# Fast matrix products in the second half of a feed-forward, and a leaner convolution transform beside them

## The chip, the cores and the metric

The kernel runs on one core of one Trainium2 chip. The metric is the device time of one execution in microseconds (us). The kernel before takes 1298.86 us, the median of three runs (1296.42 to 1302.47).

Five engines work side by side, each through its own queue in order: TensorE (PE in the profile) multiplies matrices, VectorE (DVE) and ScalarE (ACT) do elementwise work, GpSimd (POOL) issues DMAs that add to memory, SyncE (SP) issues plain DMAs. The order of each queue is fixed when the kernel is built.

## The reference

`x` is 2048 rows by 1024 columns, `F` is 3584. Two branches are summed onto `x`:

```python
xn = _layernorm(x)
# branch A, per channel, along the 2048 rows
kv  = short_causal_conv(k, shift_k, 4 taps) * v
y   = irfft(rfft(kv, 4096) * rfft(ssm_k, 4096))[:2048] + kv * ssm_D
A   = xn * y
# branch B
B   = silu(xn @ w1) @ w2        # 1024 -> 3584 -> 1024
out = x + A + B
```

All of it is float32 to the outside. The kernel multiplies matrices in float16 parts: each operand is split into a high and a low half, and a product takes three matrix multiplications (high by high, high by low, low by high).

## The kernel before, in words

**The feed-forward** has two halves. The first (`xn @ w1`, then silu) works on pairs `i` of 128-column tiles of `F` (14 pairs) and on four blocks `b` of 512 rows. Pairs 0 and 1 are partly done plainly (`plain_unit`). The rest go through `units` (line 795): two row blocks by two column tiles by two halves of the depth are a 2 by 2 block product, done with seven products in place of eight (Winograd's form; `PRODUCTS` names the seven left and right factors). The factors of `xn` and `w1` are sums formed beforehand. A unit is seven runs of 12 matmuls (P1, P7, P6, P2, P5, P3, P4), in three banks of PSUM; `evacuate` (line 722) copies parts between them with ScalarE and adds two with VectorE, and `block` (line 704) applies silu, splits the result into float16 halves (`split`, line 276: one ScalarE and one VectorE instruction) and stores it in DRAM (`hs`).

The second half (`h @ w2`) is plain in the kernel before (lines 841 to 879): for two halves `h` of 512 output columns and sixteen row tiles `t`, 28 tiles of `F` by three matmuls of 512 columns (lines 868 to 870) build one bank. `load_h` (line 903) brings `hs` back into the ring `wo`, and `norms_w2`/`load_w2` (lines 938 and 971) bring `w2`, split it with the factor `tau` and put it into the eight large `places`, which the first half has used before. `result` (line 895) copies a finished bank out with ScalarE and adds it to `out` with an accumulating DMA of GpSimd (`G`, line 250).

**The convolution** (`convolution`, line 989) runs over eight groups `g` of 128 channels beside the feed-forward. `gate` forms `kv` on VectorE. `signal_parts` transposes and splits it. `stage1` (line 1105) multiplies by the transform's constants `cfw`: for each of four `t` and two `c`, two products `p0`, `p1` of three matmuls go into two PSUM tiles, and `to_spec` (line 1137) makes their sum and difference, with one ScalarE copy and two VectorE operations. `forward`, `product` (line 1186) and `inverse` are VectorE work on the tile `spec`: butterflies, the complex product with the filter's transform, butterflies back. `energy` sums the squares for a scale. `result_parts` splits into `zh`, `zl`, `stage1_inv` (line 1317) multiplies by `civ` into the PSUM tile `py`, and `gated` (line 1338) multiplies by the normalised rows on VectorE into one of two buffers `yt`, which two accumulating DMAs of 128 KB each add to `out`. `spec` and `tmp` are single tiles, so a group's transform cannot start before the group ahead has given them up.

**The order of the work.** The class `Order` is a planner that runs at build time. Every piece is a generator that yields operations; each has an engine, a cost, a latency, a margin `m` that is kept between the end of what it reads and its own start, and a bias of its stream. The planner takes the operation that can start first, less its bias, and appends it to its engine's queue. `Ring` hands out buffers when the planner's clock frees them. A plain or accumulating DMA is priced with a fixed latency and a common pipe; an accumulating one (`G`) holds GpSimd for 1.1 us in the plan. On the chip the queues run in that order, whatever the real durations are. `places` are the eight large tiles that hold the factors of `xn`, then `w2`; the last result of the kernel waits for the convolution's results in the plan and leaves by a plain DMA (`last_result`, line 882).

Of the kernel before, what the change touches and what calls it, by code (L numbers as in the profile page):

```python
# [11 lines left out]
F32 = mybir.dt.float32  # L12
# [30 lines left out]
W2PLACE = [(5, 4, 2, 7, 6, 3, 0), (1, 5, 4, 2, 7, 6, 3)]  # L43
# [142 lines left out]

class Ring:
# [25 lines left out]
def h3_ffn_kernel(ctx, tc, x, kp, vs, fs, shift, dskip, w1, w2, cfwd, cinv, out):  # L213
# [70 lines left out]
    dram = ctx.enter_context(tc.tile_pool(name="dram", bufs=1, space=bass.MemoryType.DRAM))  # L284
    hs = [dram.tile([4, P, NF, 2, P], F16, name=f"hs{b}") for b in range(4)]
# [10 lines left out]
    wsc = cst.tile([P, NP, 4], F32, name="wsc")  # L296
    e1s = wsc[:, :, 3]
    powers = cst.tile([P, 4], F32, name="powers")
    for n, e in enumerate((14 - 64, 10 - 64, 64 - 23, 64)):
        nc.vector.memset(powers[:, n:n + 1], 2.0 ** e)  # L300
# [310 lines left out]
    def scales_w1():  # L611
        for n, (_, i) in enumerate(pairs):
# [14 lines left out]
            def then(e, i=i):  # L627
                sc = wsc[:, i]
                nc.vector.tensor_scalar(sc[:, 2:4], powers[:, 2:4], e, None, op0=MUL)
                nc.vector.reciprocal(e, e)  # L630
                nc.vector.tensor_scalar(sc[:, 0:2], powers[:, 0:2], e, None, op0=MUL)
# [71 lines left out]

    def block(i, b, j, src, tok):

        if src.space == bass.MemoryType.PSUM:
            yield hfs.ready
            hf, htok = hfs.tile([P, 4, P])
            yield a_act(hf, src, AF.Silu, wsc[:, i, 2:3])
            tok.set()  # L710
        else:
            hf, htok = src, tok
            yield a_act(hf, src, AF.Silu, wsc[:, i, 2:3])
# [81 lines left out]
    def units():  # L795
# [5 lines left out]
        for n, (i, sp) in enumerate(todo):  # L801
            if sp == 1:
                flag["unit", i].set()
            made, seen = defaultdict(Token), defaultdict(Token)
# [36 lines left out]
    def feed_forward():  # L841
# [9 lines left out]
        second["tok"].set()  # L851
        yield from units()
        flag["gemm1"].set()
        for h in range(2):
            for t in range(NT):
                yield ff.ready
                po, tok = ff.tile([P, W])
                final = (h, t) == (1, NT - 1)
                if final:
                    add(last_result(h, t, po, tok), EB)  # L860
                for c in range(NF // 4):
                    yield flag["h", h, t, c]
                    hx, htok = flag["h", h, t, c].what
                    yield flag["w2", h, c]
                    wc, wtok = w2c[h, c]
                    for jj in range(4):
                        def mm(jj=jj, j=4 * c + jj):
                            nc.tensor.matmul(po, hx[:, jj, 0, :], wc[:, jj, 0, :], start=(j == 0), stop=False)  # L868
                            nc.tensor.matmul(po, hx[:, jj, 0, :], wc[:, jj, 1, :], start=False, stop=False)  # L869
                            nc.tensor.matmul(po, hx[:, jj, 1, :], wc[:, jj, 0, :], start=False, stop=(j == NF - 1))  # L870
                        yield T(mm, po, [hx[:, jj], wc[:, jj]], 3 * 0.2185)
                    htok.set()
                    if t == NT - 1:
                        wtok.set()
                if final:
                    flag["last"].set()
                else:
                    add(result(h, t, po, tok), EB)

    flag["conv out"] = Token(NG * 4 * 2)  # L880

    def last_result(h, t, po, tok):

        yield flag["conv out"]
        yield hfs.ready
        o, otok = hfs.tile([P, W])
        to = orr[t // T2, t % T2, :, h * W:(h + 1) * W]
        yield L(o, to)
        yield flag["last"]
        yield v_stt(o, po, invc[:, 0:1], o, MUL, ADD)  # L890
        tok.set()
        yield L(to, o)
        otok.set()
# [9 lines left out]
    def load_h():  # L903
        yield flag["factors"]
        for h in range(2):
            for t in range(NT):
                for c in range(NF // 4):
                    yield wo.ready
                    flag["h", h, t, c].what = o, _ = wo.tile([P, 4, 2, P], F16)
                    yield L(o, hs[t // 4][t % 4][:, 4 * c:4 * c + 4])  # L910
                    flag["h", h, t, c].set()
# [26 lines left out]
    def norms_w2():  # L938
# [10 lines left out]
        def then(e):  # L949
            nc.vector.tensor_scalar(invc, e, 2.0 ** (64 - 25), None, op0=MUL)  # L950
            nc.vector.reciprocal(cc, e)
            nc.vector.tensor_scalar(tau, e1s, 2.0 ** (15 - 64), cc, op0=MUL, op1=MUL)
        yield from norm(ctxs["nm"], qs, (1,), then, ([invc, tau, cc], [flag["tau"]]))
        add(load_w2(), 0.05)
        for h in range(2):
            for c in range(NF // 4):
# [6 lines left out]
                for a in range(4):  # L963
                    j = 4 * c + a
                    yield lambda: bool(w2raw)
                    raw, tok = w2raw.pop(0)
                    add(split(wc[:, a, 0, :], wc[:, a, 1, :], raw, tau[:, j // 2:j // 2 + 1], (tok, flag["w2", h, c])), 0.05)

    w2raw = []

    def load_w2():
        for h in range(2):
            for j in range(NF):
                r = (ctxs["wraw"], ctxs["w2n"], hfs)[j % 3 if h == 1 and j > 3 else j % 2]
                yield r.ready
                raw, tok = r.tile([P, W])
                yield L(raw, w2r[:, j, h * W:(h + 1) * W])
# [484 lines left out]
```

## Time and profile before

| | before |
|---|---|
| median of three runs, us | 1298.86 |
| the profiled execution, us | 1299.35 |
| span of the profile, us | 1297.6 |
| mean granted TensorE clock | 0.993 |
| PE busy, share of the span | 98% |
| DVE busy | 1145.9 us, 88% |
| ACT busy | 691.9 us, 53% |
| POOL busy | 98.4 us, 8% |
| first half's last matmul starts | 607.8 us |
| second half's first matmul starts | 608.1 us |

The profile is one execution on the chip. A group of instructions is given by source line, engine, operation, the tiles it writes and reads, its shape, its count, its summed time, the mean of one in nanoseconds, and the idle time of the engine ahead of it with what ended it. Matmuls are pipelined, so the 380 ns of one matmul is its latency, and the distance from start to start is shorter. VectorE's instructions overlap a little as well.

### The profile page before, as it was taken

To read this page: it belongs to the slowest core of one execution; us is meant where nothing else is said; L and a number is where in the kernel's file an instruction comes from. 1 tells how busy PE (TensorE), PEld (TensorE's weight loads), DVE (VectorE), ACT (ScalarE), POOL (GpSimd) and SP (SyncE) were. 2 spreads that over 40 slices of the span, in tenths; PEclk is the share of its full clock that TensorE was granted. 3 is DMA by queue.
4 is the path that set the end of the run, shared out by engine and by line. 5 is a ranking of instruction groups with operands and counts; after the bars stand their busy time and mean duration, and the time that the engine had idled before them with its cause. 6 is when DMAs were issued, how large, how long until landed. Compare 5 with 4: busy or idle time off the path is not lost.

```text
span 1297.6 us, 17976 instructions
## 1 busy us (share of the span) xinstructions
PE 1268.9 (98%) x6242; PEld 618.4 (48%) x6242; DVE 1145.9 (88%) x1758; ACT 691.9 (53%) x1238; POOL 98.4 (8%) x101
## 2 busy tenths in 40 slices
PE   7899999999999998999999999999999999999998
PEld 6444544444444543445444544544544454454453
DVE  8999997889999759999899899899899989989920
ACT  6867987887766856768523412512562252241120
POOL 0000000000000011001100200210110021011021
PEclk8999999999999998999999999999999999999999
DMA  9456899789998879869954664674596367456462
GB/s 324 163 163 211 291 318 311 255 263 348 323 324 284 273 214 285 262 207 296 294 168 100 148 186 136 151 191 129 137 290 190 97 156 190 111 112 133 114 138 33
DMA packets 207003, 269.93 MB, mean 208 GB/s; under 512 B 15416, under 2 KB 121920, under 8 KB 204480
## 3 DMA queue, kind: packets, MB, share of 16 engines
q1 hardware_dynamic: 185040, 252.26, 60.7%
q0 software_dynamic: 21872, 16.52, 10.3%
q8 instruction: 49, 0.80, 0.2%
q14 instruction: 42, 0.34, 0.1%
HBM read 193.22 MB, written 83.89 MB: 214 GB/s over the span
## 4 chain that ended last, share of the span: by engine, by line
PE 71%; DVE 17%; DMA 6%; issue 4%; ACT 2%; POOL 0%; SPq 0%; DVEq 0%; ACTq 0%; POOLq 0%
PE ff L763 12%; PE ff L761 12%; PE ff L762 12%; PE ff L869 9%; PE ff L870 9%; PE ff L868 9%; DVE spec L255 5%; DVE tmp L255 3%; DVE acc L258 2%; DMA out<-yt 2%; DMA kin<-in_kp 1%; DVE x L258 1%; PE ps L1127 1%; PE ps L1129 1%; PE ps L1128 1%
## 5 line engine op out<-in xcount | busy, mean ns | idle before, releaser
L869 PE MATMUL ff<-x,wo 128*128 128x512 f16 x896 | 340.7, 380 | 1.3 <-DVE x L258 1.3
L868 PE MATMUL ff<-x,wo 128*128 128x512 f16 x896 | 340.5, 380 | 0.8 <-ACT x L266 0.8
L870 PE MATMUL ff<-x,wo 128*128 128x512 f16 x896 | 340.5, 380 | 0.0
L761 PE MATMUL ff<-x,wo 128*128 128x512 f16 (+1 forms) x808 | 305.1, 378 | 5.7 <-ACT v L266 4.2
L762 PE MATMUL ff<-x,wo 128*128 128x512 f16 (+1 forms) x808 | 305.0, 377 | 2.1 <-DVE x L258 2.1
L763 PE MATMUL ff<-x,wo 128*128 128x512 f16 (+1 forms) x808 | 304.8, 377 | 2.1 <-DVE wo L258 2.1
L255 DVE TENSOR_TENSOR spec<-spec 128x512 f32<-128x512 f32 (+2 forms) x192 | 219.4, 1175 | 1.3
L870 PEld LDWEIGHTS <-wo 128*128 128x128 f16 x896 | 87.7, 98 | 107.7 <-issue 2.4
L868 PEld LDWEIGHTS <-wo 128*128 128x128 f16 x896 | 88.6, 99 | 101.1 <-issue 0.8
L869 PEld LDWEIGHTS <-wo 128*128 128x128 f16 x896 | 87.7, 98 | 102.2 <-issue 1.7
L252 POOL DMA_DIRECT2D out<-yt x64 | 70.5, 1102 | 810.2 <-DMA w2n<-in_w 430.9
L763 PEld LDWEIGHTS <-wo 128*128 128x128 f16 x808 | 79.4, 98 | 99.5 <-DVE wo L258 4.7
L762 PEld LDWEIGHTS <-wo 128*128 128x128 f16 x808 | 79.4, 98 | 92.4 <-issue 6.4
L761 PEld LDWEIGHTS <-wo 128*128 128x128 f16 x808 | 80.6, 100 | 88.5 <-ACT wo L266 2.1
L255 DVE TENSOR_TENSOR tmp<-spec 128x512 f32<-128x512 f32 (+1 forms) x112 | 100.3, 915 | 0.2
L258 DVE SCALAR_TENSOR_TENSOR ht<-hf,wsc,ht 128x512 f16<-128x512 f32 x112 | 83.4, 746 | 17.9 <-ACT ht L266 17.6
L266 ACT ACTIVATE ht<-hf,wsc 128x512 f16<-128x512 f32 x112 | 80.9, 722 | 3.6
L258 DVE SCALAR_TENSOR_TENSOR acc<-kin,taps,acc 128x512 f32<-128x512 f32 x96 | 71.7, 747 | 2.1 <-ACT acc L266 1.9
L266 ACT ACTIVATE xg<-xg,nmr,rstd 128x128 f32<-128x128 f32 x128 | 54.8, 482 | 34.9 <-DMA xg<-in_x 33.5
L266 ACT ACTIVATE zh<-spec,csc 128x1024 f16<-128x1024 f32 x32 | 36.1, 1142 | 66.4 <-DVE spec L258 49.1
L266 ACT ACTIVATE yt<-spec 128x1024 bf16<-128x1024 f32 x32 | 33.7, 1053 | 67.6 <-DVE spec L255 67.4
L266 ACT ACTIVATE v<-ff,invc 128x512 f32<-128x512 f32 x31 | 21.2, 683 | 89.5 <-PE ff L870 89.5
(151 smaller groups left out, 1756.2 us busy)
## 6 DMA issues: line engine op xcount, KB each, us to landing
wo<-hs SPq DMA_DIRECT2D x224, 256.0 KB, 3.0
hs<-ht SPq DMA_DIRECT2D x112, 256.0 KB, 4.6
ws<-wo SPq DMA_DIRECT2D x84, 256.0 KB, 3.6
wo<-ws SPq DMA_DIRECT2D x84, 256.0 KB, 3.7
w2n<-in_w SPq DMA_DIRECT2D x80, 256.0 KB, 4.7
raw<-in_w SPq DMA_DIRECT2D x28, 512.0 KB, 5.5
kin<-in_kp SPq DMA_DIRECT2D x32, 448.0 KB, 3.7
xt<-in_x SPq DMA_DIRECT2D x16, 512.0 KB, 7.2
```

Source lines behind the costliest of these rows:

```text
L252: return Op("POOL", 1.1, 4.0, lambda: nc.gpsimd.dma_start(o, i, accum_op=ADD), [i], [o], m, n)
L255: return V(lambda: nc.vector.tensor_tensor(o, a, b, op=op), o, [a, b], **k)
L258: return V(lambda: nc.vector.scalar_tensor_tensor(o, a, s, b, op0=op0, op1=op1), o, [a, b] + ([] if isinstance(s, float) else [s]), **k)
L266: nc.scalar.activation(o, i, func, scale=scale, **kw)
L761: nc.tensor.matmul(o, w[:, 0, k], xf[:, :, k, 0], start=first and k == 0, stop=False, **kw)
L762: nc.tensor.matmul(o, w[:, 0, k], xf[:, :, k, 1], start=False, stop=False, **kw)
L763: nc.tensor.matmul(o, w[:, 1, k], xf[:, :, k, 0], start=False, stop=last and k == KH - 1, **kw)
L868: nc.tensor.matmul(po, hx[:, jj, 0, :], wc[:, jj, 0, :], start=(j == 0), stop=False)
L869: nc.tensor.matmul(po, hx[:, jj, 0, :], wc[:, jj, 1, :], start=False, stop=False)
L870: nc.tensor.matmul(po, hx[:, jj, 1, :], wc[:, jj, 0, :], start=False, stop=(j == NF - 1))
L1127: nc.tensor.matmul(ps, cf[:, 0, cs], hi[:, i], start=True, stop=False)
L1128: nc.tensor.matmul(ps, cf[:, 0, cs], lo[:, i], start=False, stop=False)
```

## The change

It has three parts.

**Fast products in the second half.** The pairs 6, 7, 8 and 9 of the 14 (eight of the 28 tiles of `F`) are taken out of the plain sum. For them the 2 by 2 blocks are two row blocks, the two tiles of a pair, and the two halves of the output columns; each of eight tiles `u` of 128 rows by two takes seven runs of 12 matmuls (`units2`). The left factors are sums of silu's results: `quad` forms them with four VectorE additions and seven splits per pair and row half, in place of four splits, and stores them in `hsf`. Silu's results wait in a tile taken from place 4 (first row half) and place 5 (second). The right factors are sums of `w2` blocks, formed in `norms_w2` after the plain part's `w2`, from raw blocks loaded again where they are needed twice. `evacuate2` empties the banks: four results per `u` go to `out` by accumulating DMAs, beside one for each of the 32 plain tiles, now of 20 tiles of `F`. The plain tiles `t` 0 and 1 of the first column half, and 14 and 15 of the second, are computed together.

**Convolution.** In stage 1 both products of a pair go into one PSUM tile, the second on top of the first; ScalarE copies twice the first before, and their sum after, and VectorE makes the difference: two ScalarE copies and one VectorE operation in place of one and two. `product` does its multiplications in four instructions of 2048, 512, 512 and 1024 elements in place of seven (one of 1024, six of 512), and `energy` writes its unused squares into `spec`, no longer into a `yt` buffer.

**Hops.** The margin of the stage 1 matmuls, forward and inverse, is 1.0 in place of 2.0; `py` may take a spare feed-forward bank, the split parts may take an `ht` buffer once the first half is over, and spare banks end with the plain part (`last part`).

In core, cut at "...":

```diff
+PAIRS = (6, 7, 8, 9)
+PLAIN = [j for j in range(NF) if j // 2 not in PAIRS]
+NC = len(PLAIN) // 4
+W2PLACE = [(5, 4, 2, 7, 6), (3, 0, 1, 5, 4)]
+FPLACE = (2, 7, 6, 3, 0, 1, 5, 4)
...
+    def quad(i, sp):
+        def factor(name, hf, tok=None):
+            yield hts.ready
+            ht, ttok = hts.tile([P, 4, 2, P], F16)
+            yield from split(ht[:, :, 0, :], ht[:, :, 1, :], hf, wsc[:, i, 2:3], () if tok is None else (tok,))
+            yield L(hsf[sp][name][:, :, PAIRS.index(i)].rearrange("q p h s -> p q (h s)"), ht.rearrange("p q h s -> p q (h s)"))
...
+        yield v_tt(v, z, v, ADD)
+        add(factor("S1", v, vt), 0.03)
+        yield v_tt(z, x, z, SUB)
+        add(factor("S3", z, zt), 0.03)
+        yield v_tt(x, v, x, SUB)
+        add(factor("S2", x, xt), 0.03)
+        yield v_tt(y, y, x, SUB)
+        add(factor("S4", y, yt), 0.03)
...
+    def units2():
+        def product2(n, u, o, first=False):
+            yield flag["h2", u, n]
+            hx, htok = flag["h2", u, n].what
+            yield flag["w2f", n]
+            wc, wtok = w2f[n]
+            yield from steps2(o, hx, wc, first, True, not first)
...
+    def evacuate2(u, one, c, made, seen):
+        def copied(src, tok, to):
+            yield hfs.ready
+            o, otok = hfs.tile([P, W])
+            yield a_act(o, src, AF.Copy, invc2[:, 0:1])
+            tok.set()
+            yield G(to, o)
+            otok.set()
...
+        yield a_act(d, two, AF.Copy, invc2[:, 0:1])
+        seen["P5"].set()
+        yield v_stt(d, c[0], invc2[:, 0:1], d, MUL, ADD)
+        seen["P7"].set()
+        yield G(at(u, 1, 1), d)
...
+        yield v_stt(a, c[0], invc2[:, 0:1], a, MUL, ADD)
+        c[1].set()
+        yield L(at(u, 1, 0), a) if last else G(at(u, 1, 0), a)
...
+        for k, (name, (_, of)) in enumerate(PRODUCTS.items()):
+            r = places[FPLACE[k + 1]]
+            yield r.ready
+            wc, wtok = w2f[name] = r.tile([P, NQ, 2, W], F16)
...
+                if of == "T3":
+                    b12, t12 = yield from next_w2()
+                    yield v_tt(src, raw, b12, SUB)
...
+                elif of == "T4":
+                    yield v_tt(src, raw, src, SUB)
...
+                elif of == "T1":
+                    b11, t11 = yield from next_w2()
+                    yield v_tt(raw, raw, b11, SUB)
...
-            yield a_act(total, p0, AF.Copy)
-            tok0.set()
-            yield v_tt(diff, total, p1, SUB)
-            yield v_tt(total, total, p1, ADD)
-            tok1.set()
+            yield a_act(diff, ps, AF.Copy, 2.0)
+            seen.set()
+            yield made
+            yield a_act(total, ps, AF.Copy)
+            yield v_tt(diff, diff, ps, SUB)
+            tok.set()
...
+                yield v_tt(run(tmp, 0, 16), steps_of(xx, 0, (2 * P, 4), (0, 4)), run(k, 0, 4, (4 * P, 2), (0, 2)), MUL)
+                for s in range(2):
+                    yield v_tt(steps_of(k, (4 * s + 3) * P, (-P, 2), (-2 * P, 2)),
+                               steps_of(xx, (4 * s + 3) * P, (0, 2), (-2 * P, 2)),
+                               steps_of(k, (4 * s + 2) * P, (-2 * P, 2), (0, 2)), MUL)
+                o = steps_of(tmp, P, (2 * P, 8))
+                yield v_tt(o, o, run(k, 0, 8), ADD)
...
-                    yield py_r.ready
-                    py, tok = py_r.tile([P, 2, 2, P])
+                    yield lambda: py_r.ready() or spare()
+                    py, tok = (py_r if py_r.ready() else ff).tile([P, 2, 2, P])
...
-                        yield T(mm, py[:, :, i, :], [hi[:, i], lo[:, i]], 0.66, m=2.0)
+                        yield T(mm, py[:, :, i, :], [hi[:, i], lo[:, i]], 0.66, m=1.0)
```

How the queues change, counted in the order of the two kernels: TensorE has 96 matmuls of 512 columns fewer. VectorE has, of 512 elements, 64 additions fewer in stage 1 and 128 multiplications or additions fewer in `product` (which has 32 more of 2048 instead), and 16 more additions on `w2` and 32 in `quad`; 24 more splits in `quad`, 12 more on `w2`, and 16 in `evacuate2`. GpSimd has 63 accumulating DMAs of 256 KB in place of 31, beside the same 64 of 128 KB.

More of the change, by code (lines that the diff above doesn't have):

```diff
@@ L854, in feed_forward @@
         for h in range(2):
-            for t in range(NT):
-                yield ff.ready
[L857 to L878, printed above, removed]
```

349 lines of the change are left out of this document (260 added, 89 removed).

## The prediction, made before the changed kernel was run

> **What bounds the kernel now.** I read first the page's line of busy times, then the stretches of the span, to see which engine has room in which stage.
>
> ```profile
> PE 1268.9 (98%) x6242; PEld 618.4 (48%) x6242; DVE 1145.9 (88%) x1758; ACT 691.9 (53%) x1238; POOL 98.4 (8%) x101
> ```
>
> ```profile
> 0.00:150.00 150.00, 135.07 (x719) 74.58 (x720) 141.33 (x317) 116.44 (x201) 0.69 (x6) 0.98 0.67 224
> 150.00:608.00 458.00, 452.65 (x2185) 215.62 (x2184) 411.02 (x643) 348.17 (x635) 13.36 (x12) 0.99 0.89 283
> 608.00:1237.00 629.00, 624.54 (x3056) 300.45 (x3054) 587.22 (x793) 220.40 (x392) 73.81 (x73) 1.00 0.62 162
> 1262.00:1290.00 28.00, 28.00 (x131) 12.63 (x130) 0.00 (x0) 0.69 (x1) 3.98 (x4) 1.00 0.30 44
> ```
>
> Behind the stretch's length stand the busy times of PE, weight loads, DVE, ACT and POOL with counts, then the granted clock, the DMA share and GB/s. PE has work throughout. In the last row 131 matmuls of 512 columns, alone, take 28.0 us, so one costs 0.2155 us (28 by 130 distances), although its own latency is 0.38. DVE idles 9, 47 and 42 us in the first three stretches, and has nothing to do after 1258. So PE sets the time now, with DVE close behind. Second I read the waits and the places where PE lost time.
>
> ```profile
> PE ff L761 <- ACT v L266: 4.2, 1, 4.2
> DVE yt L258 <- DMA out<-yt: 22.0, 5, 6.9
> ```
>
> ```profile
> 488.00:500.00 12.00, 7.80 (x24) 2.80 (x22) 11.97 (x15) 8.87 (x20) 2.87 (x3) 0.72 1.05 278
> 960.00:985.00 25.00, 22.88 (x99) 9.80 (x98) 24.88 (x31) 12.79 (x23) 1.75 (x2) 0.93 0.86 284
> ```
>
> One wait of 4.2 us at 489 drops the clock to 0.72 over 12 us: it costs 4.2 plus half of some 6 us, 7 in all. At 960 to 985, the turn between the two column halves, PE loses 2.1 us and 0.07 of 25 us more: 4. Third I read the end.
>
> ```profile
> 1239.75 1.11 POOL L252 DMA_DIRECT2D out<-yt  x1 [3.77 <-DVE yt L258]
> 1244.08 1.09 POOL L252 DMA_DIRECT2D out<-yt  x1 [3.22 <-issue]
> ...
> 1268.24 1.09 POOL L252 DMA_DIRECT2D out<-yt  x1 [2.50 <-issue]
> 1268.83 1.42 POOL L252 DMA_DIRECT2D out<-v  x1
> ```
>
> ```profile
> 1147.94 0.75 DVE L258 SCALAR_TENSOR_TENSOR yt<-py,csc,xg 128x512 f32<-128x512 f32 x1 [0.42 <-PE py L1333]
> ...
> 1166.02 0.75 DVE L258 SCALAR_TENSOR_TENSOR yt<-py,csc,xg 128x512 f32<-128x512 f32 x1 [2.53 <-PE ff L870]
> ```
>
> ```profile
> 1238.58 0.75 DVE L258 SCALAR_TENSOR_TENSOR yt<-py,csc,xg 128x512 f32<-128x512 f32 x1 [2.98 <-PE py L1333]
> ...
> 1256.03 0.75 DVE L258 SCALAR_TENSOR_TENSOR yt<-py,csc,xg 128x512 f32<-128x512 f32 x1 [6.90 <-DMA out<-yt]
> 1293.66 0.75 DVE L258 SCALAR_TENSOR_TENSOR hf<-ff,invc,hf 128x512 f32<-128x512 f32 x1 [36.88 <-PE ff L870]
> ```
>
> A group's eight accumulating DMAs go one by one, 4.07 us apart (28.5 by 7), though the instruction holds POOL for 1.1. With two buffers, a group's fourth gate (`yt`) follows the first by 17 to 18 us. At the kernel's end this is hidden now: the last group's eight are issued by 1268, PE ends at 1293.6, and 4.0 us for one addition and one plain DMA make the span.
>
> **The change, part by part.**
>
> *TensorE.* 96 matmuls less at 0.2155: **-20.7 us**. Stage 1 and the inverse keep their matmuls.
>
> *The turn at 960.* Of five pieces of the second `w2` half only two, not six, wait for places that the first half still holds. I take **-4**, bounds -4 and 0.
>
> *VectorE, in total.*
>
> ```profile
> L255 DVE TENSOR_TENSOR spec<-spec,ps 128x512 f32<-128x512 f32 x73 | 49.9, 684 | 9.1 <-PE ps L1129 7.1 <-ACT spec L266 1.1
> L258 DVE SCALAR_TENSOR_TENSOR ht<-hf,wsc,ht 128x512 f16<-128x512 f32 x112 | 83.4, 746 | 17.9 <-ACT ht L266 17.6
> L255 DVE TENSOR_TENSOR spec<-spec 128x2048 f32<-128x2048 f32 x24 | 54.9, 2287 | 0.4
> L255 DVE TENSOR_TENSOR tmp<-spec 128x1024 f32<-128x1024 f32 x48 | 58.3, 1221 | 0.2
> ```
>
> ```profile
> 1196.81 1.29 DVE L255 TENSOR_TENSOR spec<-tmp 128x512 f32<-128x512 f32 x2
> ```
>
> Two additions of 512 take 1.29 us together, one 0.69, so behind another one costs 0.60; by the same overlap a split's half costs 0.66, an operation of 1024 1.14, of 2048 2.2. Stage 1: 64 by 0.60, -38.4. `product`: 7 operations (1.14 + 6 by 0.60 = 4.74) become 2.2 + 1.2 + 1.14 = 4.54, 32 times: -6.4. Added: 48 additions, 28.8; 36 splits, 23.8; 16 results, 10.6. **Net +18 us of VectorE**, in a span that is to be 21 shorter; bounds +12 (if the strided forms overlap more) and +25. By place: in the order of the queues, VectorE's work ahead of the last addition of the first half sums to 575 us (before 553, beside 552 busy by 608 in the rows), against a TensorE queue of 580 (before 575). VectorE's idle time up to there, 56 us before, must shrink to 38 or PE waits. Part of the 56 is waits that quads can fill (the 17.6 above is a wait for ScalarE), part is gates waiting for the DMAs. I take **+5**, bounds 0 and 17.
>
> *ScalarE* gets some 80 us more; in the row of 608 to 1237 it is idle for 409 us, and in the first half, 348 of 458, the cover is thinner. I cost it at nothing; if it is late, its price falls under the +5, since the same queues meet there.
>
> *The first fast tile.* The seven right factors are split last, while stage 1 of group 7 and the product of group 6 go on. In VectorE's new queue, between the scale reduction of group 7's input (which waits for a small matmul) and the last split of T4 stand 13 operations of 512, two of 1024, one of 2048, 17 split halves or the like and seven small ones at 0.16: 7.8 + 2.3 + 2.2 + 11.3 + 1.1 = 24.7 us. TensorE's queue between that small matmul and the use of T4 (P4 of the first `u`) holds 84 matmuls and 12 transposes: 18.1 + 1.3 = 19.4. So PE waits 5 us there at least, if VectorE is on time at the start. It will not be: group 5's four gates stand ahead, with only 7 us of VectorE work among them in the new queue, and the rows above give them 17 to 18. The raw blocks, 36 where the plain form loads 16, come through four buffers. A wait of this length also costs clock, as at 489. I take **+10**, bounds 5 and 20.
>
> The Trainium skill, in "TensorE: Matmul & The Clock Gate", section "The HAM clock gate", says that an idle window of some 3.4 us sends the clock to half. The trace agrees: the 4.2 us wait above is followed by a clock of 0.72. By that rule two waits of 3 us here would cost 6 and not 10.
>
> *The end.* In the new TensorE queue the last group's first inverse block begins 22 us ahead of the queue's end (56 before), and its last block is followed by 42 matmuls, 9 us (192 before, 41). So the first accumulating DMA starts 22 less 1.3 (the block), 0.3, 0.75 (the gate) and 0.4 ahead of PE's end E: E - 19. Eight of them take 28.5 to the last issue. Behind them in the new queue stand three of 256 KB from the last `u`.
>
> ```profile
> out<-yt POOLq DMA_DIRECT2D x64, 128.0 KB, 4.1
> out<-v POOLq DMA_DIRECT2D x31, 256.0 KB, 4.4
> ```
>
> The first follows the last `yt` at once, as at 1268.83; whether two more fit is not shown. If they do: 0.6 + 0.9 + 0.9 + 4.4 = 6.8 to the last landing; if they wait for a landing, 9.5. I take 8. The end is E - 19 + 28.5 + 8 = E + 17 against E + 4 now: **+13**, bounds +5 (the inverse placed as now, only the three behind) and +17.
>
> The Trainium skill, in "DMA: Bandwidth & Descriptors", section "Anatomy of one DMA — SWDGE (gpsimd) path", fits 2.0 us plus the bytes by 436 GB/s to one DMA from GpSimd: 2.3 us for 128 KB. By that estimate the eight would end some 12 us sooner and the time be near 1291. The rows differ: 4.07.
>
> *ScalarE's wider share of stage 1, the hops at 1.0.* A shorter margin can only bring a matmul closer to what it waits for. The stage 1 matmuls wait for nothing in the rows of before; I cost the margin at nothing, bounds -2 and +6, the latter one wait of about 1 us per group.
>
> **Sum:** -20.7 - 4 + 5 + 10 + 13 = +3.3 us. The profiled execution took 1299.35 (its span 1297.6 and 1.75 around it), 0.5 above the median of 1298.86. So I forecast **1303 us**: nothing gained, the saving given back at the first fast tile and by GpSimd's queue at the end.
>
> **The rivals.**
>
> *The saving comes through in part.* VectorE keeps up (its 42 us of idle time in the long stretch absorb the waits), and the first fast tile costs at most a few us. Then the first two gifts stay and only the end gives back: 1299.35 - 20.7 - 4 + 13 = **1288**. For it speaks that PE waited hardly at all in 600 us of such order before; against it that the 24.7 and 19.4 above are counts.
>
> *VectorE becomes the bound.* The gates decide it. With 7 us of work between the first and the fourth gate where they take 17 to 18, VectorE stands 10 to 11 us per group; before, the 18.1 us from first to fourth gate held some 13 of work by the order, so 5. For groups 2 to 6 that is 5 by 6 = 30 us more standing, on top of the 18 of work. PE is spared as long as VectorE's lead covers it; the lead fell by 17 at the end of the first half, so it decides from there on. If half of the 30 reaches PE: 1303 + 15 = **1318**. For it speaks the 6.90 in the last gate's row, and the 4.2 at 489, which came by way of such a gate; against it, that most of TensorE's queue behind the gates is feed-forward that needs nothing of VectorE.
>
> *The accumulating DMAs overlap.* POOL holds each for 1.1 us, so at the least eight would start within 9 us in place of 28.5, and the end would be E + 4 again: 1303 - 13 = 1290. The rows of 4.07 speak against it; I give it 0.05, counted with the saving in part.
>
> *The change doesn't do what it says.* It does: the counts of the matmuls, stage 1 additions and product operations stand in the queues. What it can fail to do is make the hops shorter, since the margin sits in the plan and the gates in GpSimd's DMAs; then the group time stays at some 100 us and the sum above is unchanged.
>
> **How the numbers follow.** The forecast's own range, 1296 to 1311, has half of the chance; the saving in part (1278 to 1296) 0.25; VectorE as the bound (1311 to 1330) 0.25. 0.5% is 6.5 us, about what a measurement of this kernel can tell from no change: 1292.4 to 1305.4 counts as the same. Below it lie four fifths of the second case, 0.20; above it the third case and two fifths of the first, 0.45; between them 0.35. The range that leaves out a tenth on each side goes from 1286 (the second case, with the bound of 5 us at the end taken half) to 1320 (the third, a little above its price).
>
> **What would show it.** In the profile of the changed kernel: 6146 matmul records or so and VectorE busy for 1158 to 1171 us; PE waiting for VectorE on an `x` tile (the factors of `w2`) or on the last group's transposes for 5 us or more, at the first fast tile, with the clock below 1 behind it; the eight `out<-yt` of the last group some 4 us apart, the first about 19 us ahead of PE's last matmul; the last event of the span an `out<-hf` DMA of GpSimd, 12 us or more after PE's last matmul. It would be wrong if the last event were again the plain DMA 4 us after PE; if PE had no wait over 3 us in the second half; or if the accumulating DMAs came closer than 3 us.

## The result, and the profile after

The changed kernel takes **1316.51 us** (median of four runs, 1314.44 to 1317.76) against 1299.55 us (four runs, 1296.42 to 1302.47): ratio 1.0127, 95% interval 1.011 to 1.0144. It is 17 us slower. The forecast was 1303, its range 1286 to 1320.

The page's line of busy times of the kernel after:

```profile
PE 1255.1 (96%) x6146; PEld 610.2 (46%) x6146; DVE 1166.1 (89%) x1701; ACT 769.4 (59%) x1379; POOL 126.3 (10%) x133
```

The 96 matmuls are gone and VectorE has 20 us more work, yet the span grew by 15.0, from 1297.6 to 1312.6. The stretches of the kernel after (columns as in the prediction):

```profile
150.00:613.00 463.00, 452.72 (x2174) 215.42 (x2173) 424.61 (x645) 360.50 (x666) 13.35 (x12) 0.99 0.89 286
613.00:1237.00 624.00, 611.45 (x2976) 292.52 (x2975) 558.41 (x689) 272.28 (x482) 92.95 (x95) 0.99 0.71 183
1128.00:1142.00 14.00, 7.86 (x36) 3.42 (x35) 14.00 (x19) 9.01 (x15) 1.74 (x2) 0.95 0.82 222
960.00:985.00 25.00, 25.00 (x118) 11.33 (x116) 22.65 (x23) 7.14 (x16) 6.17 (x6) 1.00 0.80 174
1237.00:1313.00 76.00, 55.78 (x283) 27.44 (x280) 41.87 (x52) 20.25 (x32) 19.29 (x20) 0.90 0.58 98
```

The turn at 960 to 985 now has PE busy for all of its 25 us: that stall is gone. At the first fast tile (1128 to 1142) PE works 7.86 of 14 us while VectorE works all 14. In the last 76 us PE is busy for 55.78. The waits of the kernel after (engine, line, who ended the wait; us in total, times, longest):

```profile
PE py L1581 <- DVE yt L285: 5.7, 2, 3.6
...
PE ff L976 <- DVE x L285: 3.3, 5, 1.1
PE px L1355 <- DVE ht L285: 3.2, 1, 3.2
...
DVE yt L285 <- DMA out<-yt: 30.4, 6, 7.0
```

VectorE stands 30.4 us (22.0 before) at gates whose buffer an accumulating DMA still holds. The timeline of the kernel after at its end, first VectorE's last gates, then GpSimd's queue:

```profile
1271.73 0.75 DVE L285 SCALAR_TENSOR_TENSOR yt<-py,csc,xg 128x512 f32<-128x512 f32 x1 [0.43 <-PE py L1583]
...
1275.63 0.75 DVE L285 SCALAR_TENSOR_TENSOR yt<-py,csc,xg 128x512 f32<-128x512 f32 x1
1283.40 0.75 DVE L285 SCALAR_TENSOR_TENSOR yt<-py,csc,xg 128x512 f32<-128x512 f32 x1 [7.01 <-DMA out<-yt]
1290.78 0.75 DVE L285 SCALAR_TENSOR_TENSOR yt<-py,csc,xg 128x512 f32<-128x512 f32 x1 [6.63 <-DMA out<-yt]
```

```profile
1272.93 1.11 POOL L279 DMA_DIRECT2D out<-yt  x1 [1.85 <-DVE yt L285]
1277.22 1.09 POOL L279 DMA_DIRECT2D out<-yt  x1 [3.17 <-issue]
1277.79 1.43 POOL L279 DMA_DIRECT2D out<-v  x1
...
1301.52 1.09 POOL L279 DMA_DIRECT2D out<-yt  x1 [2.35 <-issue]
1302.09 1.44 POOL L279 DMA_DIRECT2D out<-hf  x1
1305.03 0.87 POOL L279 DMA_DIRECT2D out<-w  x1 [1.49 <-issue]
1305.57 1.22 POOL L279 DMA_DIRECT2D out<-hf  x1
```

The eight `out<-yt` go out over 28.6 us, 4.1 apart, and three larger ones follow. PE's last matmul starts at 1295.3, so the span ends 17.3 us after it.

To compare all kernels I use one measure: for each matmul the distance to the start of the next, less the median distance of the matmuls of its line. Its sum over a stretch of the profiled execution is what PE **lost** there, clock included. "Tail" is the time from the start of PE's last matmul to the end of the span, and "median" is that of all runs. All in us:

| kernel | median | lost to 150 | 150–605 | 605–660 | 660–1100 | 1100–1160 | after 1160 | tail |
|---|---|---|---|---|---|---|---|---|
| before | 1299.6 | 10.3 | 7.5 | 0.0 | 6.3 | -0.2 | -0.2 | 4.4 |
| after | 1316.5 | 10.6 | 15.5 | 1.2 | 6.2 | 10.8 | 3.1 | 17.3 |
| e1: after, 1408 bytes | 1288.7 | 10.9 | 12.5 | 0.8 | -0.3 | 6.8 | 0.8 | 5.8 |
| e11: after, 1152 bytes | 1289.9 | 10.9 | 10.9 | 0.5 | 0.0 | 7.0 | 0.8 | 8.8 |
| e4: before, 1408 bytes | 1290.0 | 10.5 | 3.1 | 0.0 | 1.4 | -0.2 | -0.2 | 4.3 |
| e2: convolution part | 1326.4 | 11.0 | 17.5 | 9.2 | 8.1 | 3.3 | 1.9 | 4.3 |
| e5: e2, 1408 bytes | 1303.7 | 8.5 | 8.1 | 9.4 | 0.6 | 0.2 | -0.1 | 4.3 |
| e6: e2, margin 2.0 | 1310.8 | 8.3 | 13.0 | 8.2 | 4.1 | 0.7 | -0.1 | 4.4 |
| e3: fast products alone | 1345.9 | 10.2 | 10.8 | 0.0 | 10.3 | 14.2 | 23.3 | 22.3 |
| e9: after, margin 2.0 | 1340.6 | 10.6 | 18.1 | 0.0 | 4.1 | 13.4 | 21.4 | 22.1 |
| e10: e9, 1408 bytes | 1311.5 | 12.8 | 16.4 | 0.0 | -0.7 | 10.0 | 13.4 | 11.4 |
| e7: e1, sums ahead | 1287.6 | 9.1 | 11.8 | 0.7 | 0.5 | 6.5 | 0.8 | 5.7 |
| e8: e1, no left sums | 1294.5 | 8.0 | 9.6 | 12.6 | 1.8 | 5.6 | 0.9 | 4.5 |
| e12: e1, sums on GpSimd | 1303.2 | 8.4 | 11.3 | 0.4 | 3.7 | 20.5 | 0.7 | 4.8 |

What is left when the losses are taken off PE's last start is 1269.5 before and 1247.8 after: 21.7 less. (Some lines have matmuls of two widths. With a median for each width it is 19.7 less, and what is lost up to 150 us is some 10 us more in every kernel; the other columns move by less than 1.) Against the 21.7 stand +0.3 up to 150 us, +8.0 at 150–605, +1.2, -0.1, +11.0, +3.3 and +12.9 of tail, 36.6 in all. The difference is +14.9, and the span grew by 15.0. So the gain came, and all of it and more was given back, the largest part at the tail.

### The profile page after: what moved, and what is told of

Its sections match the earlier page's. It is cut to its first block, busy times and chain, and to the rows that moved or that the text cites. A ratio compares the mean times of both kernels' runs of the same rounds, so it can differ in the third digit from the quotient of the medians.

```text
span 1312.6 us, 17986 instructions
## 1 busy us (share of the span) xinstructions
PE 1255.1 (96%) x6146; PEld 610.2 (46%) x6146; DVE 1166.1 (89%) x1701; ACT 769.4 (59%) x1379; POOL 126.3 (10%) x133
## 4 chain that ended last, share of the span: by engine, by line
PE 43%; DVE 34%; issue 11%; DMA 7%; ACT 3%; POOL 2%; SPq 0%; POOLq 0%; DVEq 0%; ACTq 0%
DVE spec L282 10%; PE ff L851 7%; PE ff L849 7%; PE ff L850 7%; PE ff L976 6%; PE ff L977 6%; PE ff L975 5%; DVE tmp L282 5%; DVE ht L285 3%; DVE acc L285 3%; DVE x L285 2%; DMA out<-yt 2%; POOL out L279 2%; DVE spec L285 2%; DVE wo L285 1%
## 5 line engine op out<-in xcount | busy, mean ns | idle before, releaser
L976 PE MATMUL ff<-x,wo 128*128 128x512 f16 x864 | 328.4, 380 | 3.3 <-DVE x L285 3.3
L975 PE MATMUL ff<-x,wo 128*128 128x512 f16 x864 | 328.4, 380 | 1.5 <-ACT w L293 0.8
L977 PE MATMUL ff<-x,wo 128*128 128x512 f16 x864 | 328.4, 380 | 0.0
L282 DVE TENSOR_TENSOR spec<-spec 128x512 f32<-128x512 f32 (+2 forms) x256 | 261.7, 1050 | 1.7
L977 PEld LDWEIGHTS <-wo 128*128 128x128 f16 x864 | 84.7, 98 | 106.8 <-issue 5.7
L975 PEld LDWEIGHTS <-wo 128*128 128x128 f16 x864 | 85.6, 99 | 97.5 <-issue 1.1
L976 PEld LDWEIGHTS <-wo 128*128 128x128 f16 x864 | 84.7, 98 | 99.4 <-issue 3.2
L851 PEld LDWEIGHTS <-wo 128*128 128x128 f16 x808 | 79.4, 98 | 98.5 <-issue 4.1
L850 PEld LDWEIGHTS <-wo 128*128 128x128 f16 x808 | 79.4, 98 | 96.6 <-issue 11.1
L849 PEld LDWEIGHTS <-wo 128*128 128x128 f16 x808 | 80.7, 100 | 86.9 <-issue 1.1
L282 DVE TENSOR_TENSOR tmp<-spec 128x2048 f32<-128x2048 f32 (+1 forms) x48 | 92.5, 1932 | 0.9
L285 DVE SCALAR_TENSOR_TENSOR ht<-hf,wsc,ht 128x512 f16<-128x512 f32 x104 | 76.4, 744 | 6.6 <-ACT ht L293 6.5
L293 ACT ACTIVATE ht<-hf,wsc 128x512 f16<-128x512 f32 x104 | 74.6, 719 | 6.8 <-DVE hf L282 4.5
L293 ACT ACTIVATE wo<-raw,wsc 128x512 f16<-128x512 f32 x84 | 59.3, 711 | 15.0 <-DVE raw L282 15.0
L279 POOL DMA_DIRECT2D out<-v x39 | 36.7, 940 | 308.1 <-ACT v L293 274.8
L293 ACT ACTIVATE spec<-spec 128x1024 bf16<-128x1024 f32 x32 | 33.7, 1055 | 55.3 <-DVE spec L282 55.2
L285 DVE SCALAR_TENSOR_TENSOR wo<-raw,wsc,wo 128x512 f16<-128x512 f32 x84 | 61.9, 742 | 3.4 <-ACT wo L293 3.2
```

Source lines behind the costliest of these rows:

```text
L279: return Op("POOL", 1.1, 4.0, lambda: nc.gpsimd.dma_start(o, i, accum_op=ADD), [i], [o], m, n)
L282: return V(lambda: nc.vector.tensor_tensor(o, a, b, op=op), o, [a, b], **k)
L285: return V(lambda: nc.vector.scalar_tensor_tensor(o, a, s, b, op0=op0, op1=op1), o, [a, b] + ([] if isinstance(s, float) else [s]), **k)
L293: nc.scalar.activation(o, i, func, scale=scale, **kw)
L849: nc.tensor.matmul(o, w[:, 0, k], xf[:, :, k, 0], start=first and k == 0, stop=False, **kw)
L850: nc.tensor.matmul(o, w[:, 0, k], xf[:, :, k, 1], start=False, stop=False, **kw)
```

## The experiments

**e1 and e4: room for GpSimd's DMAs.** The theory after the result: the program gives GpSimd's DMAs 1024 bytes (`dynamic_dma_scratch_size`), too little for two `out<-yt` at once, so that they go one by one and hold the gates' buffers. One number is changed, in the changed kernel (e1) and in the kernel before (e4):

```diff
-    nc = bacc.Bacc("TRN2", target_bir_lowering=False, num_devices=1, dynamic_dma_scratch_size=1024)
+    nc = bacc.Bacc("TRN2", target_bir_lowering=False, num_devices=1, dynamic_dma_scratch_size=1408)
```

> The changed kernel with 1408 in place of 1024 bytes for the descriptors of GpSimd's DMAs, nothing else. Theory (the accumulating DMAs wait for room for their descriptors, and that makes the gates stand and the end long): two of 128 KB go out together, the distance falls from 3.7-4.0 us to 2.5 or less, the last DMA is issued some 10 us sooner after the first gate, the gates' waits for out<-yt (30 us in the changed kernel) fall by half, and the time goes from 1316 to about 1302. Rival (each waits for the landing of the one before because both add to the same rows, or the transfer itself takes 3.7 us): distance and time unchanged, 1316.

> The kernel before with 1408 bytes for the descriptors. Theory: its accumulating DMAs are off the path at the end (issued by 1268, PE ends at 1293), so only the stop at 489 can go: 1292 to 1299. Rival (gates' waits hold VectorE and so everything): 1285 or less.

e1: **1288.65 us**, ratio to before 0.9914 (0.9894 to 0.9934), 28 us less than the changed kernel. e4: 1289.98, ratio 0.9921 (0.9904 to 0.9939), 10 us less than before. The waits of e1, and its GpSimd queue at the end (x2 marks two issues in one row):

```profile
DVE yt L285 <- DMA out<-yt: 6.4, 2, 4.1
```

```profile
1259.08 2.22 POOL L279 DMA_DIRECT2D out<-yt  x2 [1.90 <-DVE yt L285]
1261.49 0.89 POOL L279 DMA_DIRECT2D out<-v  x1 [0.19 <-issue]
1263.51 2.23 POOL L279 DMA_DIRECT2D out<-yt  x2 [1.13 <-DVE yt L285]
...
1274.20 1.10 POOL L279 DMA_DIRECT2D out<-yt  x1 [0.42 <-issue]
...
1278.05 0.88 POOL L279 DMA_DIRECT2D out<-hf  x1 [0.95 <-ACT hf L293]
```

Two now go out together, and the eight take 15.1 us in place of 28.6. The landings say the same of the whole run: in the two kernels with 1024 bytes none of the 64 `out<-yt` is issued before the one ahead of it has landed (54 of them within 0.5 us after that in the changed kernel, 55 in the one before), and in e1 52 are. (With 1024 bytes a larger `out<-v` does go out beside an `out<-yt`, as at 1277.79 above.) VectorE's wait at the gates falls from 30.4 to 6.4 us, the tail from 17.3 to 5.8, and PE loses 16 us less ahead of it (31.5 against 47.5 in all). The direction was as expected, the size larger: I had counted the tail and little of the gates. e4 falls between its theory (1292 or more) and its rival (1285 or less): besides the stop at 489, which is gone (4.4 us less lost at 150–605), 4.9 us come back at 660–1100, where I had expected nothing.

With room for both kernels the change is worth next to nothing: 1288.65 against 1289.98, and the two ratios' intervals overlap. The table tells where its 22 us then go: 9 more are lost at 150–605, 7 at 1100–1160, 1 after it, and the tail is 1.5 longer, while 1.7 less are lost at 660–1100.

**e11: how much room.** The changed kernel with 128 bytes more:

```diff
-    nc = bacc.Bacc("TRN2", target_bir_lowering=False, num_devices=1, dynamic_dma_scratch_size=1024)
+    nc = bacc.Bacc("TRN2", target_bir_lowering=False, num_devices=1, dynamic_dma_scratch_size=1152)
```

> The whole change with 1152 bytes of descriptor room: 128 more than the kernel has, a third of what 1408 adds. Theory (what decides is whether the descriptors of two 128 KB accumulating DMAs fit together, and 1024 is just short of it): a step, 1286 to 1293 us. Rival (every byte counts, or two fit only near 1408): 1300 to 1318 us.

1289.94 us (1287.7 to 1290.4), ratio 0.9932 (0.991 to 0.9954). It is a step, between 1024 and 1152 bytes.

**e2: the convolution part alone.** The convolution section of the change, hops included, with the second half plain as before:

```diff
-        def to_spec(g, t, total, diff, p0, tok0, p1, tok1):
+        def to_spec(g, t, total, diff, ps, seen, made, half, tok):
...
-                            yield T(mm, ps, [hi[:, i], lo[:, i]], 0.65, m=2.0)
+                            yield T(mm, ps, [hi[:, i], lo[:, i]], 0.65, m=1.0)
...
-                        yield T(mm, py[:, :, i, :], [hi[:, i], lo[:, i]], 0.66, m=2.0)
+                        yield T(mm, py[:, :, i, :], [hi[:, i], lo[:, i]], 0.66, m=1.0)
```

> The kernel before with the convolution's part of the change alone (stage 1 joined in PSUM, the wider product, the hops at 1.0, the spare banks), second half plain. It takes 64 additions and the narrow product operations from VectorE, about 45 us, and nothing from TensorE. Theory (TensorE bounds the kernel before): 1292 to 1300, the convolution ending earlier beside it. Rival (VectorE bounds it already): 1280 or less.

**1326.44 us**, ratio 1.0206 (1.018 to 1.0232). Both expectations fall: VectorE has 42 us less work and the kernel is 26 us slower. The waits of e2:

```profile
PE ff L869 <- DVE x L258: 6.5, 6, 1.5
PE py L1337 <- DVE yt L258: 6.5, 3, 5.1
...
PE ps L1145 <- DVE spec L255: 4.1, 4, 2.6
...
DVE yt L258 <- DMA out<-yt: 44.9, 9, 9.0
```

The gates are planned closer together than their DMAs go, so VectorE stands at them for 44.9 us where it stood for 22.0, and PE meets it late at the transforms and at the factors of `w2`.

**e5 and e6: which of the two, room or margin.** e5 is e2 with 1408 bytes; e6 is e2 with the old margin:

```diff
-                            yield T(mm, ps, [hi[:, i], lo[:, i]], 0.65, m=1.0)
+                            yield T(mm, ps, [hi[:, i], lo[:, i]], 0.65, m=2.0)
...
-                        yield T(mm, py[:, :, i, :], [hi[:, i], lo[:, i]], 0.66, m=1.0)
+                        yield T(mm, py[:, :, i, :], [hi[:, i], lo[:, i]], 0.66, m=2.0)
```

> The convolution part of the change alone (second half plain), with 1408 bytes of descriptor room for GpSimd's DMAs in place of 1024. The same part with 1024 bytes took 1326 us, PE losing 51 us between its matmuls against 24 in the kernel before. Theory (the gates now stand closer together than two accumulating DMAs take, VectorE stands at them, and PE behind it): with room for three the loss falls to 15 to 25 us, 1287 to 1300 us. Rival (the hops are planned too close to their producers, whatever the DMAs do): 1312 us or more.

> The convolution part of the change alone, with 1024 bytes as before, but the margin of the stage 1 matmuls back at 2.0. Theory (the gates and their DMAs cost the 27 us, the margin does not): still 1315 to 1332 us. Rival (the closer hops cost it): 1305 us or less.

e5: 1303.72 us, ratio 1.0029 (1.0015 to 1.0044). e6: 1310.82, ratio 1.0079 (1.0064 to 1.0094). The room takes away 23 of the 26 us and the margin alone 16: both expectations of the theory are missed by a few us, and for the margin I was wrong. The gates stand less when the hops lie further apart. The waits of e6, then of e5:

```profile
DVE yt L258 <- DMA out<-yt: 36.3, 7, 9.3
```

```profile
PE ff L869 <- DVE x L258: 2.7, 4, 1.1
...
DVE yt L258 <- DMA out<-yt: 14.6, 3, 5.0
```

What is left in e5 against e4, 14 us, lies at two places: 5 us at 150–605 and 9 us at 605 to 660, where the second half begins. That stretch in e5, then in e4:

```profile
605.00:660.00 55.00, 49.23 (x216) 21.68 (x215) 53.89 (x70) 26.71 (x45) 0.88 (x1) 0.94 0.86 276
```

```profile
605.00:660.00 55.00, 55.00 (x256) 24.95 (x255) 49.55 (x59) 23.98 (x45) 3.94 (x4) 1.00 0.87 266
```

VectorE is full there in e5 (53.89 of 55), and PE waits for the factors `x` of `w2`: 2.7 us in four waits for VectorE's half of them (L869) and 2.4 us in two waits for ScalarE's (L868); the clock is 0.94. In e5 the transform of a group begins earlier than in e4 and falls on the start of the second half; its first butterfly in e5, then in e4:

```profile
606.19 2.28 DVE L255 TENSOR_TENSOR spec<-spec 128x2048 f32<-128x2048 f32 x1
```

```profile
627.51 2.28 DVE L255 TENSOR_TENSOR spec<-spec 128x2048 f32<-128x2048 f32 x1
```

That this place causes the loss is not shown. Where the transform begins at 602 (e8), 606 (e5) and 614 us (e2), 9 to 13 us are lost, and where it begins at 620 (e1) and 627 (e4), at most 0.8. But in e6 it begins at 632.6, later than in any of these, and 8.2 us are lost, again in waits for `x`:

```profile
632.60 2.28 DVE L255 TENSOR_TENSOR spec<-spec 128x2048 f32<-128x2048 f32 x1
```

What the four kernels with the loss share is the wait for these factors; why they come late stays open.

**e3: the fast products alone.** The changed kernel with the convolution section of before, margins of 2.0 included:

```diff
-        def to_spec(g, t, total, diff, ps, seen, made, half, tok):
+        def to_spec(g, t, total, diff, p0, tok0, p1, tok1):
...
-                            yield T(mm, ps, [hi[:, i], lo[:, i]], 0.65, m=1.0)
+                            yield T(mm, ps, [hi[:, i], lo[:, i]], 0.65, m=2.0)
...
-                        yield T(mm, py[:, :, i, :], [hi[:, i], lo[:, i]], 0.66, m=1.0)
+                        yield T(mm, py[:, :, i, :], [hi[:, i], lo[:, i]], 0.66, m=2.0)
```

> The changed kernel with the convolution of before (stage 1 with two tiles, the narrow product, hops at 2.0); the spare banks still end with the plain part. VectorE has some 45 us more than in the changed kernel, 63 more than before, TensorE 20.7 us less. Theory (VectorE's queue and the convolution's end set the time of the changed kernel): 1335 to 1360, with the end moved out by the convolution. Rival (the time is given back at the first fast tile and by the three DMAs behind the last gate alone, whatever VectorE has to do): 1316 within 5.

**1345.92 us**, ratio 1.0352 (1.0324 to 1.0379), as the theory had it. So neither part gains by itself (+45 and +26), and together they cost 17. The last two stretches of e3:

```profile
1237.00:1290.00 53.00, 52.22 (x245) 23.77 (x243) 52.31 (x63) 12.92 (x21) 9.56 (x12) 1.00 0.60 107
1290.00:1340.00 50.00, 10.36 (x51) 6.12 (x49) 19.92 (x29) 8.37 (x13) 9.69 (x9) 0.65 0.32 49
```

The feed-forward's last matmul starts at 1290, and then PE works 10 of 50 us: the last group of the convolution ends behind it, alone.

**e9 and e10: the margin in the whole change.** The same two lines as in e6, in the changed kernel with 1024 bytes (e9) and with 1408 (e10).

> The whole change with 1024 bytes of descriptor room, but the margin of the stage 1 matmuls, forward and inverse, back at 2.0. With the convolution part alone the shorter margin cost 16 us (1326 against 1311). Theory (closer hops cost through VectorE, which then stands at the gates and is late for its next work): 1300 to 1311 us against 1316.5. Rival (as the prediction had it, the margin is worth nothing in the whole change): 1313 to 1320 us.

> The whole change with 1408 bytes and the margin back at 2.0. Theory (with room for the descriptors VectorE hardly stands at the gates, so there is little left for the margin to cost): 1285 to 1292 us, as with 1.0 (1288.7). Rival (the closer hops cost by themselves): 1280 us or less.

e9: **1340.63 us**, ratio 1.0331 (1.0305 to 1.0357). e10: 1311.49, ratio 1.0102 (1.0079 to 1.0124). Theory and rival fall alike: here the old margin is *worse* by 24 and by 23 us, where it was better by 16 in the convolution part alone. The last stretches of e9, then the last of e10:

```profile
1237.00:1296.00 59.00, 58.22 (x271) 26.46 (x270) 57.94 (x66) 14.60 (x23) 11.27 (x13) 1.00 0.64 116
1296.00:1339.00 43.00, 11.04 (x49) 6.53 (x47) 11.68 (x13) 8.46 (x13) 9.69 (x9) 0.54 0.36 55
```

```profile
1282.00:1311.00 29.00, 10.04 (x49) 6.07 (x47) 11.83 (x13) 8.35 (x13) 9.77 (x9) 0.60 0.55 82
```

The feed-forward ends at 1295.7 in e9, as in the changed kernel (1295.3). But the last group's first gate stands at 1303.33 and not at 1271.73, 32 us later, so the last inverse runs alone, at a clock of 0.54:

```profile
1303.33 0.74 DVE L285 SCALAR_TENSOR_TENSOR yt<-py,csc,xg 128x512 f32<-128x512 f32 x1
```

With the margin at 1.0 the last inverse still lies beside the fast tiles. In the convolution part alone the last group ends 79 us ahead of the feed-forward (its last inverse matmul starts at 1239.7, the last matmul at 1318.6), so that bringing it forward gains nothing and only the crowding is left.

**e7, e8 and e12: the work on VectorE.** All three are e1 with one more edit. e7 puts the stream of the right factors first, e8 leaves out the sums of the left factors, e12 gives the right factors' additions to GpSimd.

```diff
-            for gen, bias in ((result_parts(), CB), (stage1_inv(), 0.02), (norm_rows(), 0.0), (norms_w2(), 0.03)):
+            for gen, bias in ((result_parts(), CB), (stage1_inv(), 0.02), (norm_rows(), 0.0), (norms_w2(), 0.055)):
```

> The whole change with 1408 bytes, and the stream that forms the right factors from w2 given a bias of 0.055 in place of 0.03, so that its additions and splits stand ahead of the convolution's in VectorE's queue. With 1408 bytes and the old bias it took 1288.7 us, and PE lost 7 us at the first fast tile. Theory (the last factors are late there because VectorE's queue holds convolution work ahead of them): the loss falls to 2 us or less, 1282 to 1286 us. Rival (VectorE is full from 740 to 1160 us in any order, so another wait takes its place): 1287 to 1292 us.

1287.56 us, ratio 0.9908 (0.9893 to 0.9923), the same as e1 (0.9894 to 0.9934). The rival is right: the loss at the first fast tile stays, 6.5 against 6.8. The stretch of the first fast tile in e1, then in e7:

```profile
1115.00:1131.00 16.00, 11.37 (x51) 5.49 (x49) 15.97 (x22) 10.74 (x18) 2.58 (x3) 0.89 0.85 228
```

```profile
1115.00:1131.00 16.00, 11.61 (x54) 5.36 (x52) 15.79 (x28) 11.14 (x19) 2.58 (x3) 0.93 0.86 231
```

VectorE is full in both; only who waits for it changes (in e1 mostly the last group's transposes, in e7 mostly the fast tile's matmuls).

```diff
-        yield v_tt(v, z, v, ADD)
...
-        yield v_tt(z, x, z, SUB)
...
-        yield v_tt(x, v, x, SUB)
...
-        yield v_tt(y, y, x, SUB)
```

> The whole change with 1408 bytes, without the four VectorE additions per pair and row half that form the sums of the left factors (32 additions of 0.60 us, 19 us of VectorE; the left factors are then copies of silu's results without the sums, so this part of the computation is left out). With them it took 1288.7 us. Theory (VectorE's added work in the first half is what PE loses there, 8 us beyond the kernel before without such waits, and 7 at the first fast tile): 1274 to 1282 us. Rival (the first half's waits come from the gates and the order, not from the amount of work): 1285 to 1290 us.

1294.53 us, ratio 0.9953 (0.9938 to 0.9968): 6 us more than e1 with 19 us less work. The losses at 150–605 and 1100–1160 fell as the theory has it, by 2.9 and 1.2, but 12 us more are lost at 605–660, again in waits for the factors of `w2`. The order of the queues moved with the edit; why it costs at this place is open, as told at e5:

```profile
605.00:660.00 55.00, 46.81 (x198) 19.97 (x197) 53.10 (x69) 33.59 (x57) 3.94 (x4) 0.94 0.86 264
```

As a test of the amount of work it is inconclusive.

```diff
+    def p_tt(o, a, b, op, m=0.15):
+        return Op("POOL", 1.3, 0.3, lambda: nc.gpsimd.tensor_tensor(o, a, b, op=op), [a, b], [o], m)
...
-                    yield v_tt(src, raw, b12, SUB)
+                    yield p_tt(src, raw, b12, SUB)
```

(and the same in the three other additions of `norms_w2`).

> The whole change with 1408 bytes, and the 16 additions and subtractions that form the right factors from w2 done by GpSimd in place of VectorE. Without that it took 1288.7 us, and PE lost 7 us at the first fast tile, where VectorE has no idle time for some 10 us before each factor. Theory (VectorE's amount of work ahead of the first fast tile is what PE waits for: 16 by 0.60 is 10 us less of it): the loss there falls to 3 us or less, 1281 to 1286 us. Rival (GpSimd is slower at it, its DMA issues stand between, and the factors come no earlier): 1288 to 1296 us.

1303.24 us, ratio 1.0033 (1.0018 to 1.0047): 15 us slower than e1, worse than the rival. The timeline of e12 at the first fast tile, VectorE first, then GpSimd:

```profile
1136.12 0.69 DVE L282 TENSOR_TENSOR spec<-spec 128x512 f32<-128x512 f32 x1
1136.84 6.92 DVE L282 TENSOR_TENSOR tmp<-tmp,spec 128x1024 f32<-128x1024 f32 x1
```

```profile
1136.53 1.58 POOL L285 TENSOR_TENSOR x<-wraw,x 128x512 f32<-128x512 f32 x1
1137.89 1.43 POOL L285 TENSOR_TENSOR x<-w2n,x 128x512 f32<-128x512 f32 x1
1139.11 1.43 POOL L285 TENSOR_TENSOR x<-wraw,x 128x512 f32<-128x512 f32 x1
1140.32 1.05 POOL L279 DMA_DIRECT2D out<-hf  x1
1140.94 1.73 POOL L285 TENSOR_TENSOR x<-w2n,x 128x512 f32<-128x512 f32 x1
```

An addition of VectorE that takes 1.22 us elsewhere lasts 6.92, until GpSimd's four are done, and PE waits for what stands behind it:

```profile
PE px L1358 <- DVE ht L288: 8.8, 1, 8.8
```

The Trainium skill, in "SBUF — State Buffer", section "Who interferes with whom", says that a VectorE instruction with two inputs in SBUF contends with a GpSimd instruction that reads SBUF, and that the shared pair of ports is an exclusive lock. This trace agrees, and shows more: VectorE's addition waited for all four of GpSimd's, though three of them began after it, and it was the same at 1084.79, where one of VectorE's lasted 6.51 us beside four of GpSimd's.

## Why the prediction was right or wrong

The time lies in the range and on the slower side; the forecast was 13.5 us low. The profiled execution took 1314.4, so the steps below can account for 11.7 of them: the sum was +3.3 and the span grew by 15.0. By its steps:

- **TensorE, -20.7: right.** The span without PE's losses fell by 21.7 (19.7 with a median for each width).
- **The turn at 960, -4: right in itself** (25.00 busy of 25). But at 660–1100 as a whole PE lost 6.2 after and 6.3 before: about 4 came back in small waits of stage 1 and its transposes, which the sum had at nothing. I had put such waits under the hops, with a bound of +6. Of the 4 the margin explains some 2 (with the old one, e9, 4.1 of the 6.2 are still lost there). With 1408 bytes these waits are gone (-0.3 in e1), so they hang on the DMAs' room.
- **VectorE in the first half, +5: too low**, 9.2 with the start of the second half, inside the bounds of 0 and 17. Busy time, 1166.1, lies in the 1158 to 1171 given.
- **The first fast tile, +10: right**, 11.0. VectorE was full and PE waited for `x` and for the last group's transposes, as described. The waits add up to 7.2 us, the longest 3.24; the rest is clock, 0.50 at 1142 to 1146 and 0.81 at 1146 to 1150. So the lower price of 6, two waits of 3 us that leave the clock alone, did not hold. 4 of the 11 go with the room (6.8 left in e1).
- **The end, +13: the mechanism right, the equal number (12.9) partly luck.** The eight `out<-yt` are 4.1 us apart, and the last event is an `out<-hf`. What the step left out: the same DMAs hold the last two gates for 7.01 and 6.63 us, and PE lost 3.3 us ahead of its last matmul, so that the first `out<-yt` starts 22.7 us ahead of PE's end and not 19. And behind the last `out<-yt` the span goes on for 11.1 us, not 8: the second of the three larger DMAs was issued at 1305.03, after that `out<-yt` had landed (1304.71). The two errors nearly cancel in the tail; with the 3.3 the end costs 16.2.
- **Rivals.** "VectorE becomes the bound" came nearest with its 1318, and its mechanism was there: gates that stand on DMAs and reach PE. It was smaller than its price: the room takes 16 us of PE's losses from the changed kernel and 9 from the one before, so the change adds 7 us by the gates where the rival had 15. These 7 are no term beside the others: against the kernel before they lie at the first fast tile (4.0), after 1160 (2.3) and at 660–1100 (1.6). What the sum lacks of the 11.7 is 4.2 in VectorE's first half, 3.9 at 660–1100 and 3.3 ahead of the last matmul. "The accumulating DMAs overlap", priced at 1290, is false at 1024 bytes and true at 1152 and more, where the kernel takes 1288.7 to 1289.9.
- **The tail by the rows, 4.07 us each, and by the Trainium skill.** "DMA: Bandwidth & Descriptors", section "Anatomy of one DMA — SWDGE (gpsimd) path", gave 2.3 us for 128 KB, and my estimate from it a time near 1291. The traces don't agree: no `out<-yt` lands less than 3.1 us after its issue (median 4.1 before, 3.9 after, 4.4 in e1). In the changed kernel the rows were right. With 1408 bytes the eight are 2.2 us apart since two are under way at once, not since one takes 2.3; that 1288.7 lies near 1291 is luck.

What I had not seen at all is what the margin is for. I costed it at nothing because I took the place of the last group from the order of the changed kernel, where the shorter margin is already in. Without it the change would take 1340.6. The three parts depend on each other: the fast products shorten TensorE's queue and load VectorE, so that the convolution ends last (e3, e9); the closer hops bring it forward (24 us). They crowd the gates in the convolution part alone (44.9 us of standing in e2, 36.3 in e6), but not in the whole change, where the gates stand 57.4 us with the old margin (e9) and 30.4 with the new one.

Partly open: why the loss at 150–605 is 9 us higher with the change even with room (e1 against e4). Two single waits of PE, which e4 doesn't have, make up 7 of it. One is 3.24 us for VectorE's `hf` at 252.8; without the quads' sums (e8) it is gone. The other is 3.74 us at 482.05, behind a gate that VectorE starts at 481.24, just after an `out<-yt` issued at 474.20 has landed (481.17): that one took 7.0 us, so a gate can stand with room too. Why it took so long was not tried. Also untried alone are the other parts of the hops, the spare bank for `py` and the `ht` buffers, which e2, e5 and e6 all have.

The fastest versions are e7 and e1, 1287.6 and 1288.7, about 12 us below the kernel before and 28 below the changed one. e4 comes within 1 to 2 us of them by the 384 bytes alone.

## What to carry to other kernels

When accumulating DMAs of one queue go one at a time, each issued just after the one ahead has landed, look for what they wait for before planning around it: here 128 bytes of room were worth 27 us to the changed kernel, more than the 22 that its 96 matmuls saved. Taking work from the busiest engine shows in the time only if the chain that then ends last is short too, so read the last event of each stream, not only the busiest engine. An order fixed at build time moves as a whole with each edit: compare parts alone and together, and by stretches, before a part is called good or bad.

## What the runs showed of the hardware

- GpSimd's accumulating DMAs of 128 KB, from one queue: 4.1 us apart with `dynamic_dma_scratch_size` of 1024; with 1152 and 1408 the time of the kernel is the same, 27 to 28 us less (1289.9 and 1288.7 against 1316.5). That it is the descriptors of two such DMAs that don't fit is inferred, from this step and from the landings told at e1.
- An addition of 128x512 float32 holds GpSimd for about 1.2 to 1.4 us from start to start (1136.53, 1137.89, 1139.11), twice VectorE's 0.60, and stops a VectorE addition beside it (6.92 us in place of 1.22).
